# Gate and value products of a gated layer by Strassen's algorithm, with combined weights made early and streamed from DRAM

## The chip, the cores and the metric

The kernel runs on one core of one Trainium2 chip. The metric is the device time of one execution in microseconds (us). Every text below that speaks of an engine uses the profile's names: PE is TensorE (PEld its weight loads), DVE is VectorE, ACT is ScalarE, POOL is GpSimd, SP is SyncE, which here only issues DMAs.

## The reference: what is computed

Three stages, all in float32. Retention (linear attention with a decay) over q, k, v of 4 batches, 8 heads, 576 positions and head size 64 gives 2304 tokens of width 512. Two feed-forward layers follow:

```python
def _moe_ref(x, w_in, w_out):          # w_in 512 x 2048, w_out 2048 x 512
    h = x @ w_in
    sp = np.where(h > 20.0, h, np.log1p(np.exp(np.minimum(h, 20.0))))
    return (h * np.tanh(sp)) @ w_out
def _moe2_ref(x, w_gate, w_val, w_out):  # 512 x 1536, 512 x 1536, 1536 x 512
    g = x @ w_gate
    silu = g * (1.0 / (1.0 + np.exp(-g)))
    return (silu * (x @ w_val)) @ w_out
```

The weights arrive as 64-bit floats and are brought to 32 bits on the chip, two 32-bit words at a time.

## The kernel before

All the work of the two layers is cut into blocks of T = 384 tokens: 2304 tokens make NB = 6 blocks. Activations lie transposed, 128 features on the partitions and 384 tokens along the row. Every float32 operand of a matrix product is split into a rounded high part and a low remainder, each 32 bits wide, and a product is the sum of three: high by high, high by low, low by high. So `prod` (L424), which multiplies a 512 x 128 piece of weights with a block, issues 4 x 3 = 12 matmuls of 384 columns (L430).

**First layer.** `slot(s)` (L490) is one of 6 x 16 = 96 steps: `g1` makes 128 features of h for a block (12 matmuls), `mish` and `halves` (ACT activation, ACT cast, DVE subtraction) make and split the activation, and `g2` of four slots earlier (LAG = 4) adds its part to the block's result (12 matmuls, L464). The last slot of a block copies the result to `x2t[b]`.

**Second layer.** 6 x 12 = 72 steps (L565 on): `gv_prod` makes a gate and a value bank (24 matmuls), `silu` takes the activation on ACT (L537), multiplies on DVE (L540) and splits the product with `halves` (L486 on ACT, L487 on DVE), and `fin` of two steps earlier multiplies it with 128 rows of w_out, 9 matmuls of 512 columns (L551), into three banks that stand for a whole block. The last `g2` steps of the first layer stand between the first steps of the second. `split_x` splits the next block's activations at the end of each block.

**Weights.** `weights` (L132) takes one 512 KB raw piece through a chain: `fetch` (a DMA on SP's queue), `rebias` (ACT L102, DVE L103), `sign` (DVE L107), `join` (DVE L111), and `part` (ACT cast L125, POOL subtraction L126) into a resident tile. There are 32 pieces for the first layer, taken during retention and the first 17 slots, and 36 for the second, taken in the last two blocks of the first layer and the first eleven steps of the second, because a piece can only lie where one of the first layer has come free (pools `wa` with 19 and `wb` with 14 tiles of 4 KB a partition).

**Order.** The order on each engine is the order in the code (`manual_schedule`); each engine runs its own instructions in that order and waits on the others by semaphores. `pha` and `ph` are two banks each of PSUM, `acc` four; `bank` (L439) passes the four of `pha` and `ph` round.

Of the kernel before, what the change touches and what calls it, by code (L numbers as in the profile page):

```python
# [7 lines left out]
F32 = mybir.dt.float32  # L8
# [8 lines left out]
def retention_mish_swiglu(  # L17
# [35 lines left out]
    gp = ctx.enter_context(tc.tile_pool(name="gp", bufs=3))  # L53
    pha = ctx.enter_context(tc.tile_pool(name="pha", bufs=2, space=PSUM))


    def cols(w, i):
        return w.bitcast(U32)[:, i * 256:(i + 1) * 256].rearrange("(k p) f -> p k f", p=128)

    def rows(w, i):  # L60
        return w.bitcast(U32)[i * 128:(i + 1) * 128, :]
# [5 lines left out]
        if i >= OFF:  # L67
            todo.append(("out", i - OFF, rows(w1_out, i - OFF)))
    n1 = len(todo)
    for i in range(F2):  # L70
        todo.append(("gate", i, cols(w2_gate, i)))
        todo.append(("val", i, cols(w2_val, i)))
        todo.append(("fin", i, rows(w2_out, i)))

    NU = len(todo) - 3
    unit = {}
    pools = {"a": wa}
    raw = {}
# [2 lines left out]
    def words(j):  # L81
        w = raw[j].rearrange("p (n t) -> p n t", t=2)
        return w[:, :, 0], w[:, :, 1]
# [12 lines left out]
    def rebias():  # L96
        j = stage[1]
        if j >= stage[0]:
            return
        stage[1] += 1  # L100
        lo, hi = words(j)
        nc.scalar.activation(hi.bitcast(F32), hi.bitcast(F32), AF.Copy, scale=2.0 ** -112)  # L102
        nc.vector.tensor_scalar(lo, lo, 29, None, op0=ALU.logical_shift_right)  # L103
# [9 lines left out]
    def part(lim):  # L113
        j = stage[3]
        if j >= min(lim, stage[2]):
            return
        stage[3] += 1
        kind, i, _ = todo[j]
        where = "a" if j < NA else "b" if j < NA + NBU else "a" if j < 2 * NA + NBU else "b"
        if j < NU:  # L120
            u = pools[where].tile([128, 2, DM], F32R, tag="u", name=f"u{j}")
        else:
            u = xp.tile([128, 2, DM], F32R, tag="raw", name=f"u{j}", bufs=RAW)
# [8 lines left out]
    def weights(lim, late=False):  # L132
        j = stage[2]
        on = j < min(lim, stage[1])
        if on:
            sign(j)
        yield
        if late:
            part(lim)
        if stage[1] < seen[0]:  # L140
            rebias()
        seen[:] = seen[1], stage[0]
        yield
        if on:
            join(j)
            stage[2] += 1
        while not late and stage[3] < stage[2]:
            part(lim)
        fetch(lim + 3)
        seen[1] = stage[0]  # L150

    def run(step):
        for _ in step:
            pass

    xt = {}
    x2t = {}
    xs = {}
# [2 lines left out]
        d[j] = xp.tile([128, KT, T], F32, tag="x", name=f"{nm}{j}", bufs=5)  # L161

    def split_hi(d, nm, j, kk):
        s = xp.tile([128, 2, T], F32R, tag="xs", name=f"{nm}s{j}_{kk}", bufs=XS)
        nc.scalar.copy(out=s[:, 0, :], in_=d[j][:, kk, :])
        xs[nm, j, kk] = s

# [255 lines left out]
    with tc.manual_schedule():  # L423
        def prod(ps, u, nm, j):  # L424
            n = 3 * KT
            c = 0
            for kk in range(KT):
                s = xs[nm, j, kk]
                for a, e in ((0, 0), (0, 1), (1, 0)):
                    nc.tensor.matmul(  # L430
                        ps, lhsT=u[:, a, kk * 128:(kk + 1) * 128], rhs=s[:, e, :],
                        start=(c == 0), stop=(c == n - 1),
                    )
                    c += 1
# [55 lines left out]
        def slot(s):  # L490
            b, i = divmod(s, F1)
            if i == 0 and s:
                g2(s - LAG)
            g1(s)
            if s >= LAG and i:
                g2(s - LAG)
            d, nm, j = (xt, "x", b + 1) if b + 1 < NB else (x2t, "y", 0)
            parts = (i - F1 + 4,) if b and F1 - 4 <= i < F1 - 2 else range(2, KT) if i == F1 - 1 else ()
# [4 lines left out]
            lim = 0  # L503
            if s < F1 + OFF:
                lim = 0 if parts else n1
                while stage[3] < min(2 * s - OFF + 2 if s > OFF else s, n1):
                    run(weights(n1))
            elif b < NB - 1:
                lim = NA + NBU if i % 4 == 1 and b > 1 else 0
            elif i >= 2 and i % 6 != 5:  # L510
                lim = NA + NBU + 2 * i
# [4 lines left out]
            if lim:  # L516
                run(weights(lim, True))

        retention(slot)
        pools["b"] = ctx.enter_context(tc.tile_pool(name="wb", bufs=NBU, reuse_waits="tile"))  # L520
        pools["ph"] = ctx.enter_context(tc.tile_pool(name="ph", bufs=2, space=PSUM, reuse_waits="tile"))
        pools["acc"] = ctx.enter_context(tc.tile_pool(name="pacc", bufs=4, space=PSUM, reuse_waits="tile"))
        for s in range(2, NS):
            slot(s)


        def gv_prod(s):
            b, i = divmod(s, F2)
            ga, va = bank(f"ga{s}"), bank(f"va{s}")
            prod(ga, unit["gate", i], "y", b)  # L530
            prod(va, unit["val", i], "y", b)
            return ga, va

        def silu(s, ga, va):
            sg = gp.tile([128, T], F32, tag="w", name=f"sg{s}")
            more = stage[3] < len(todo)
            nc.scalar.activation(sg, ga, AF.Silu)  # L537
            if more:
                run(weights(len(todo)))
            nc.vector.tensor_tensor(out=sg, in0=sg, in1=va, op=ALU.mult)  # L540
            halves(sg, ("f", s))
            if more:
                run(weights(len(todo)))

        def fin(s):
            b, i = divmod(s, F2)
            if i == 0:
                accs["f", b] = [pools["acc"].tile([128, DM], F32, tag="acc", name=f"fa{b}_{d}") for d in range(TT)]
            u, g = unit["fin", i], gs.pop(("f", s))
            for m, a, e, c in order(TT, i == F2 - 1):  # L550
                nc.tensor.matmul(  # L551
                    accs["f", b][m], lhsT=g[:, e, m * 128:(m + 1) * 128], rhs=u[:, a, :],
                    start=(i == 0 and c == 0), stop=(i == F2 - 1 and c == 2),
                )
                if i == F2 - 1 and c == 2:
                    if m == 0:
                        ob = xp.tile([128, TT, DM], F32, tag="x", name=f"o{b}", bufs=5)
                    o = ob[:, m, :]
# [4 lines left out]
        NS2 = NB * F2  # L563
        nc.scalar.preload_act_table_set("silu_and_others")
        for s in range(NS2):  # L565
            b, i = divmod(s, F2)
            if s == 0:
                g2(NS - 4)
            pair = gv_prod(s)
            if s == 0:  # L570
                g2(NS - 3)
            elif s == 1:
                g2(NS - 2)
                g2(NS - 1)
                g2_out(NS - 1)
            silu(s, *pair)
            if s > 1:
                fin(s - 2)
            if b + 1 < NB and i >= F2 - 3:
                kk = i - (F2 - 3)  # L580
                if kk < 2:
                    split_x(x2t, "y", b + 1, kk, nc.vector)
                else:
                    split_x(x2t, "y", b + 1, 2, nc.vector)
                    split_x(x2t, "y", b + 1, 3, nc.vector)
        fin(NS2 - 2)
        fin(NS2 - 1)


# [56 lines left out]
```

## Time and profile before

| | us |
|---|---|
| median of three runs | 970.83 (970.68 to 971.12) |
| the profiled execution | 971.39 |
| its span in the trace | 969.6 |
| PE busy in the span | 949.1 (98%), 5900 matmuls |
| DVE busy | 366.6 (38%) |
| ACT busy | 320.5 (33%) |
| POOL busy | 139.9 (14%) |
| moved by DMA | 55.86 MB |

The page of the profile gives busy time by engine, the span in slices, the chain that ended last and the costliest groups of instructions. Matmuls overlap in the trace (one that is noted as 334 ns starts 173 ns behind the one before), so the pace of PE is read from the starts of successive groups in the timeline, not from the mean duration of one.

### The profile page before, as it was taken

How to read it: one execution, taken by the hardware profiler on the slowest of the kernel's cores; microseconds unless marked ns; L12 is line 12 of the kernel's file. 1: busy time of each engine (PE TensorE's matmuls, PEld its weight loads, DVE VectorE, ACT ScalarE, POOL GpSimd, SP SyncE). 2: the span in 40 equal slices, each digit the busy share in tenths (PEclk: the TensorE clock that was granted, in tenths of full speed). 3: DMA queues.
4: the chain of work that ended last, by engine and by line, in shares of the span. 5: the costliest groups of instructions: out<-in, count | busy, mean ns of one | idle time of the engine just before them, and what ended most of it. 6: DMA issues, size and time to landing. Idle time of an engine off the chain costs nothing.

```text
span 969.6 us, 14043 instructions
## 1 busy us (share of the span) xinstructions
PE 949.1 (98%) x5900; PEld 905.9 (93%) x5900; DVE 366.6 (38%) x575; ACT 320.5 (33%) x626; POOL 139.9 (14%) x102
## 2 busy tenths in 40 slices
PE   9898999999999999999999979999999999999998
PEld 8777899999999999999999969999999999999997
DVE  3997796212111112114686883122122122112211
ACT  4776564322322223224454542122112112112111
POOL 3765343000000000001333540000000000000000
PEclk9999999999999999999999999999999999999999
DMA  9999353000000000001334530000000000000000
GB/s 227 256 247 244 122 164 109 23 1 1 23 1 1 1 1 1 1 1 44 109 109 130 169 114 33 1 1 33 1 1 24 10 1 1 33 1 1 33 1 33
DMA packets 76848, 55.86 MB, mean 58 GB/s; under 512 B 41456, under 2 KB 70896, under 8 KB 76784
## 3 DMA queue, kind: packets, MB, share of 16 engines
q1 hardware_dynamic: 75680, 54.53, 20.5%
q8 instruction: 46, 0.75, 0.3%
q10 hardware_dynamic: 1104, 0.42, 0.2%
q14 instruction: 18, 0.15, 0.1%
HBM read 50.23 MB, written 4.72 MB: 57 GB/s over the span
## 4 chain that ended last, share of the span: by engine, by line
PE 86%; issue 3%; DVE 3%; DMA 3%; ACT 2%; POOL 2%; SPq 1%; POOLq 0%; DVEq 0%; ACTq 0%
PE h L430 21%; PE acc L464 21%; PE fa L551 14%; PE va L430 14%; PE ga L430 13%; DMA k<-in_k_dram 1%; POOL u L126 1%; PE o L356 1%; DVE raw L111 1%; DVE raw L107 1%; PE s L289 1%; PE idle L398 1%; DVE raw L103 1%; DMA raw<-in_moe_w_in_dram 1%; PE o L349 1%
## 5 line engine op out<-in xcount | busy, mean ns | idle before, releaser
L430 PE MATMUL h<-xs,u 128*128 128x384 f32 x1152 | 214.3, 334 | 0.0
L464 PE MATMUL acc<-g,u 128*128 128x384 f32 x1152 | 214.0, 334 | 0.0
L430 PEld LDWEIGHTS h<-xs,u 128*128 128x128 f32 x1152 | 200.8, 188 | 0.3 <-issue 0.2
L464 PEld LDWEIGHTS acc<-g,u 128*128 128x128 f32 x1152 | 201.0, 188 | 0.0
L430 PE MATMUL ga<-ys,u 128*128 128x384 f32 x864 | 165.2, 339 | 4.0 <-POOL u L126 2.2
L430 PEld LDWEIGHTS ga<-ys,u 128*128 128x128 f32 x864 | 154.6, 189 | 11.3 <-POOL u L126 2.8
L126 POOL TENSOR_TENSOR u<-raw,u 128x512 fp32r<-128x512 f32 x68 | 102.2, 1507 | 424.5 <-ACT u L125 397.7
L430 PE MATMUL va<-ys,u 128*128 128x384 f32 x864 | 161.9, 334 | 1.0 <-POOL u L126 1.0
L430 PEld LDWEIGHTS va<-ys,u 128*128 128x128 f32 x864 | 150.7, 188 | 1.6 <-POOL u L126 1.6
L487 DVE TENSOR_TENSOR g<-m,g 128x384 fp32r<-128x384 f32 x96 | 53.7, 559 | 255.8 <-ACT g L486 255.8
L540 DVE TENSOR_TENSOR sg<-sg,va 128x384 f32<-128x384 f32 x72 | 39.7, 552 | 260.8 <-PE va L430 260.8
L481 ACT ACTIVATE m<-h 128x384 f32<-128x384 f32 x96 | 47.3, 493 | 241.4 <-PE h L430 241.3
L537 ACT ACTIVATE sg<-ga 128x384 f32<-128x384 f32 x72 | 35.4, 492 | 174.9 <-PE ga L430 174.9
L125 ACT CAST u<-raw 128x512 fp32r<-128x512 f32 x68 | 44.9, 662 | 56.4 <-DVE raw L111 56.4
L103 DVE TENSOR_SCALAR raw<-raw 128x512 uint32<-128x512 uint32 x68 | 60.8, 895 | 1.6 <-DMA raw<-in_moe_w_out_dram 1.4
L107 DVE SCALAR_TENSOR_TENSOR raw<-raw 128x512 uint32<-128x512 uint32 x68 | 53.6, 788 | 0.0
L111 DVE SCALAR_TENSOR_TENSOR raw<-raw 128x512 uint32<-128x512 uint32 x68 | 51.0, 749 | 0.1
L486 ACT CAST g<-m 128x384 fp32r<-128x384 f32 x96 | 49.5, 515 | 2.5
L102 ACT ACTIVATE raw<-raw 128x512 f32<-128x512 f32 x68 | 46.8, 689 | 1.6 <-DMA raw<-in_moe_w_out_dram 0.9
L277 POOL TENSOR_TENSOR vs<-v,gv 128x512 f32<-128x512 f32 (+1 forms) x20 | 25.7, 1284 | 18.4 <-DMA v<-in_v_dram 14.1
L298 DVE TENSOR_TENSOR p<-s,mask 128x512 f32<-128x512 f32 (+1 forms) x40 | 23.5, 629 | 5.0 <-PE s L289 4.9
L356 PE MATMUL o<-p,vs 128*64 128x128 f32 (+1 forms) x320 | 21.3, 270 | 1.1 <-DVE p L298 1.0
(326 smaller groups left out, 682.8 us busy)
## 6 DMA issues: line engine op xcount, KB each, us to landing
raw<-in_moe_w_out_dram SPq DMA_DIRECT2D x28, 512.0 KB, 3.6
raw<-in_moe_w_in_dram SPq DMA_DIRECT2D x16, 512.0 KB, 5.2
raw<-in_moe_w_gate_dram SPq DMA_DIRECT2D x12, 512.0 KB, 3.6
raw<-in_moe_w_val_dram SPq DMA_DIRECT2D x12, 512.0 KB, 3.6
out_dram<-o SPq DMA_DIRECT2D x18, 256.0 KB, 2.3
q<-in_q_dram SPq DMA_DIRECT2D x8, 512.0 KB, 6.3
k<-in_k_dram SPq DMA_DIRECT2D x16, 256.0 KB, 5.8
v<-in_v_dram SPq DMA_DIRECT2D x16, 256.0 KB, 6.1
```

The source lines that it names most:

```text
L102: nc.scalar.activation(hi.bitcast(F32), hi.bitcast(F32), AF.Copy, scale=2.0 ** -112)
L103: nc.vector.tensor_scalar(lo, lo, 29, None, op0=ALU.logical_shift_right)
L107: nc.vector.scalar_tensor_tensor(lo, hi, 0x80000000, lo, op0=ALU.bitwise_and, op1=ALU.bitwise_or)
L111: nc.vector.scalar_tensor_tensor(lo, hi, 3, lo, op0=ALU.logical_shift_left, op1=ALU.bitwise_or)
L125: nc.scalar.copy(out=u[:, 0, :], in_=w)
L126: nc.gpsimd.tensor_tensor(out=u[:, 1, :], in0=w, in1=u[:, 0, :].bitcast(F32), op=ALU.subtract)
L430: nc.tensor.matmul(ps, lhsT=u[:, a, kk * 128:(kk + 1) * 128], rhs=s[:, e, :], start=(c == 0), stop=(c == n - 1),)
L464: nc.tensor.matmul(accs[b][d][:, :T], lhsT=u[:, a, d * 128:(d + 1) * 128], rhs=g[:, e, :], start=(i == 0 and c == 0), stop=(i == F1 - 1 an ...
L481: nc.scalar.activation(w, hs.pop(s), AF.Mish)
L486: nc.scalar.copy(out=g[:, 0, :], in_=x)
L487: nc.vector.tensor_tensor(out=g[:, 1, :], in0=x, in1=g[:, 0, :].bitcast(F32), op=ALU.subtract)
L551: nc.tensor.matmul(accs["f", b][m], lhsT=g[:, e, m * 128:(m + 1) * 128], rhs=u[:, a, :], start=(i == 0 and c == 0), stop=(i == F2 - 1 and ...
```

## The change

The gate and value products of two pieces of 128 features (e = 0, 1) and two blocks of tokens (h = 0, 1), each with the 512 rows of the sum cut into two halves of 256, are a 2 x 2 by 2 x 2 product of blocks. The changed kernel forms it with seven block products in place of eight (Winograd's form of Strassen's algorithm). A unit u of the second layer is such a pair of pieces for such a pair of blocks: 3 pairs of blocks x 6 pairs of pieces = 18 units, each with 7 products of 6 matmuls for the gate (z = 0) and 7 for the value (z = 1). Three banks t1, t2, t3 a half take turns in the two banks of `pha`; t1 and t2 and t3 are read by ACT or DVE in the middle of their accumulation, and p1, u and v are kept in SBUF.

The weights' side (a11, a12, a22 and four sums s1 to s4) is made in slots 20 to 82 of the first layer by `second`, in steps spread over five slots for each pair of pieces and side, split into high and low parts, written to DRAM and read back by `stream`, one 512 KB tile for two products, through nine buffers, anew for each pair of blocks. The activations' side (three parts as they are and four combinations) is made by `ysteps` on DVE and ACT: for the first pair of blocks in the last four slots of the first layer, for the others beside the last unit of the pair before. w_out's pieces go through DRAM too and are read once. The last four `g2` of the first layer run in a row. The matmuls of `fin` for unit u are handed out between the products of unit u + 1, two or three behind each product.

```diff
-    NA, NBU = 19, 14
+    NA, NBU = 19, 13
...
+    PREP = 20
...
-    wa = ctx.enter_context(tc.tile_pool(name="wa", bufs=NA))
+    cl, cr = ExitStack(), ExitStack()
+    wa = cr.enter_context(tc.tile_pool(name="wa", bufs=NA, side="right"))
...
+    def put(x, dst, nm, eng):
+        c = pools["c"].tile([128, 2, KH], F32R, tag="c", name=nm)
+        nc.scalar.copy(out=c[:, 0, :], in_=x)
+        eng.tensor_tensor(out=c[:, 1, :], in0=x, in1=c[:, 0, :].bitcast(F32), op=ALU.subtract)
+        nc.sync.dma_start(out=dst, in_=c.bitcast(F32))
...
+    def group(i, z, stg):
...
+        if stg == 3:
+            for out_, a, b, op in (
+                (s[1], v["a21"], v["a22"], ALU.add), (s[3], v["a11"], v["a21"], ALU.subtract),
+                (s[2], s[1], v["a11"], ALU.subtract), (s[4], v["a12"], s[2], ALU.subtract),
+            ):
+                nc.vector.tensor_tensor(out=out_, in0=a, in1=b, op=op)
+        for c, nm in enumerate(USES):
+            if (nm[0] == "a") == (stg == 3):
+                n = z * NG + c
+                put(v[nm] if nm[0] == "a" else s[int(nm[1])], comb[i][n // 2][:, n % 2], f"c{i}_{n}", nc.vector)
...
+    def second(s):
+        for n in range(2 * PAIRS):
+            t = s - PREP - 5 * n
+            if 0 <= t < 5:
+                group(n // 2, n % 2, t)
+            if 4 <= t < 8:
+                last(n, t - 4)
...
+        SA, SB = 4, 5
...
+        def stream(n):
...
+            su[n] = pools["sa" if n % (SA + SB) < SA else "sb"].tile([128, 2, 2, KH], F32R, tag="su", name=f"su{n}")
+            nc.sync.dma_start(out=su[n].bitcast(F32), in_=comb[n // NG % PAIRS][n % NG])
...
+        def ysplit(n, c, x):
+            y = pools["y"].tile([128, 2, KT // 2, T], F32R, tag="y", name=f"y{n}_{c}")
+            nc.scalar.copy(out=y[:, 0], in_=x)
+            nc.vector.tensor_tensor(out=y[:, 1], in0=x, in1=y[:, 0].bitcast(F32), op=ALU.subtract)
...
+        def ysteps(n):
...
+            ysplit(n, 0, b[1, 1])
+            minus(b[1, 1], b[1, 2], b[1, 1])
+            yield
...
+            minus(t2, b[2, 2], b[1, 1])
+            ysplit(n, 1, t2)
+            yield
+            ysplit(n, 2, b[2, 1])
+            minus(b[2, 1], b[2, 1], t2)
+            yield
+            minus(b[1, 2], b[2, 2], b[1, 2])
+            ysplit(n, 3, b[1, 2])
+            yield
+            ysplit(n, 4, b[1, 1])
+            yield
+            ysplit(n, 5, b[2, 1])
+            yield
+            ysplit(n, 6, b[2, 2])
+            yield
...
+            if s == NS - 5:
+                cr.close()
...
+                y0 = ysteps(0)
+            elif y0:
+                next(y0, None)
+                next(y0, None)
+        for s in range(NS - LAG, NS):
+            g2(s)
+            g2_out(s)
...
+        def strassen(u, z):
...
+            def result(e, h, bank_, part_):
+                if z == 0:
+                    x = pools["sg"].tile([128, T], F32, tag="sg", name=f"sg{u}_{e}{h}")
+                    if part_ is not None:
+                        add(x, bank_, part_)
+                    nc.scalar.activation(x, bank_ if part_ is None else x, AF.Silu)
+                    sg[u, e, h] = x
+                else:
+                    x = bank_
+                    if part_ is not None:
+                        x = pools["sg"].tile([128, T], F32, tag="cv", name=f"cv{u}_{e}{h}", bufs=2)
+                        add(x, bank_, part_)
+                    y = sg[u, e, h]
+                    nc.vector.tensor_tensor(out=y, in0=y, in1=x, op=ALU.mult)
+                    finish(u, e, h)
...
+            for c, (nm, tn, begin, end) in enumerate((
+                ("a11", 1, True, True), ("s2", 2, True, True), ("a12", 1, False, True), ("s3", 2, False, True),
+                ("s1", 3, True, True), ("a22", 2, False, True), ("s4", 3, False, True),
+            )):
+                if begin:
+                    t[tn] = pha.tile([128, T], F32, tag="h", name=f"t{u}_{z}_{tn}")
...
+                for kk in range(KT // 2):
+                    for a, x in ((0, 0), (0, 1), (1, 0)):
+                        nc.tensor.matmul(
+                            p, lhsT=w[:, n % 2, a, kk * 128:(kk + 1) * 128], rhs=y[:, x, kk, :],
...
+                if n % 2:
+                    stream(u * NG + n // 2 + SA + SB)
+                if c == 0:
...
+                    nc.scalar.copy(out=r["p1"], in_=p)
+                elif c == 1:
...
+                    add(r["u"], p, r["p1"])
+                elif c == 2:
+                    result(0, 0, p, None)
+                elif c == 3:
...
+                    add(r["v"], p, r["p1"])
+                elif c == 4:
+                    result(1, 1, p, r["v"])
+                elif c == 5:
+                    result(1, 0, p, r["p1"])
+                else:
+                    result(0, 1, p, r["u"])
+                fins(FINS[c])
+                if nexty and n >= 6:
+                    next(nexty[0], None)
...
+        FINS = (3, 2, 3, 2, 3, 2, 3)
```

`finish` calls `halves` on the product of silu and value and queues the nine `fin` matmuls of (e, h) for the next unit; `nexty` holds `ysteps` of the next pair of blocks in units 5 and 11.

## Rows read from the trace of the kernel before

**Rows 1.** The page: span; part 1, busy us, share, instructions.

```profile
span 969.6 us, 14043 instructions
PE 949.1 (98%) x5900; PEld 905.9 (93%) x5900; DVE 366.6 (38%) x575; ACT 320.5 (33%) x626; POOL 139.9 (14%) x102
```

**Rows 2.** Timeline of an undisturbed step of the second layer: start, us, engine, line, instructions.

```profile
704.74 2.27 PE L430 MATMUL ga<-ys,u 128*128 128x384 f32 x12
...
706.84 2.24 PE L430 MATMUL va<-ys,u 128*128 128x384 f32 x12
707.10 0.49 ACT L537 ACTIVATE sg<-ga 128x384 f32<-128x384 f32 x1 [3.07 <-PE ga L430]
...
708.92 2.24 PE L551 MATMUL fa<-u,g('f', 29)_6160 128*128 128x512 f32 x9
709.19 0.55 DVE L540 TENSOR_TENSOR sg<-sg,va 128x384 f32<-128x384 f32 x1 [4.57 <-PE va L430]
709.78 0.52 ACT L486 CAST g('f', 31)_6242<-sg 128x384 fp32r<-128x384 f32 x1 [2.19 <-DVE sg L540]
710.32 0.56 DVE L487 TENSOR_TENSOR g('f', 31)_6242<-sg,g('f', 31)_6242 128x384 fp32r<-128x384 f32 x1 [0.58 <-ACT g('f', 31)_6242 L486]
...
711.00 2.27 PE L430 MATMUL ga<-ys,u 128*128 128x384 f32 x12
```

**Rows 3.** Timeline of PE where the first layer ends and the second begins.

```profile
496.50 4.32 PE L464 MATMUL acc<-g,u 128*128 128x384 f32 x24
500.65 2.24 PE L430 MATMUL ga<-ys,u 128*128 128x384 f32 x12
...
559.05 2.27 PE L430 MATMUL ga<-ys,u 128*128 128x384 f32 x12
```

**Rows 4.** Timeline of PE where the second layer waits for its weights, and behind it.

```profile
568.22 2.01 PE L430 MATMUL ga<-ys,u 128*128 128x384 f32 x10 [1.39 <-POOL u L126]
...
576.28 0.62 PE L430 MATMUL ga<-ys,u 128*128 128x384 f32 x2 [1.89 <-ACT u L125]
...
577.67 3.38 PE L430 MATMUL ga<-ys,u 128*128 128x384 f32 x10 [0.77 <-POOL u L126]
...
585.67 2.27 PE L430 MATMUL ga<-ys,u 128*128 128x384 f32 x12
```

**Rows 5.** Stages: start:end, length, busy us (instructions) PE to POOL, granted clock, DMA share, GB/s.

```profile
200.00:300.00 100.00, 100.00 (x579) 100.00 (x578) 19.54 (x37) 28.82 (x60) 1.31 (x1) 1.00 0.02 6
...
564.00:568.00 4.00, 2.83 (x13) 1.94 (x11) 3.48 (x7) 2.49 (x5) 1.70 (x1) 1.00 0.69 243
...
576.00:578.00 2.00, 0.95 (x3) 0.63 (x4) 1.32 (x2) 1.21 (x3) 1.31 (x1) 0.82 0.00 0
578.00:580.00 2.00, 2.00 (x7) 2.00 (x7) 1.57 (x4) 0.34 (x1) 0.00 (x0) 0.50 0.00 0
580.00:582.00 2.00, 1.64 (x7) 1.33 (x7) 1.23 (x1) 1.23 (x3) 1.30 (x1) 0.83 0.00 0
```

**Rows 6.** DMA issues: KB each, median us from issue to landing.

```profile
raw<-in_moe_w_out_dram SPq DMA_DIRECT2D x28, 512.0 KB, 3.6
```

**Rows 7.** Groups by line and shape: busy us, mean ns of one, idle before.

```profile
L103 DVE TENSOR_SCALAR raw<-raw 128x512 uint32<-128x512 uint32 x68 | 60.8, 895 | 1.6 <-DMA raw<-in_moe_w_out_dram 1.4 <-DMA raw<-in_moe_w_val_dram 0.2
...
L125 ACT CAST u<-raw 128x512 fp32r<-128x512 f32 x68 | 44.9, 662 | 56.4 <-DVE raw L111 56.4
...
L165 ACT CAST ys<-y 128x384 fp32r<-128x384 f32 x24 | 11.7, 511 | 0.0
...
L369 DVE TENSOR_TENSOR x<-o,gout 128x512 f32<-128x512 f32 x14 | 9.6, 688 | 12.8 <-PE o L356 12.7
...
L369 DVE TENSOR_TENSOR x<-o,gout 128x256 f32<-128x256 f32 x8 | 3.2, 417 | 1.8 <-POOL gout L307 0.9 <-PE o L356 0.8
```

**Rows 8.** Timeline: the end of the kernel.

```profile
963.71 2.20 PE L551 MATMUL fa<-u,g('f', 71)_7948 128*128 128x512 f32 x9
```

**Rows 9.** Timeline: a DVE subtraction while POOL is at work (POOL 531.37, 1.32 us).

```profile
531.68 1.42 DVE L487 TENSOR_TENSOR g('f', 3)_4914<-sg,g('f', 3)_4914 128x384 fp32r<-128x384 f32 x1 [0.68 <-ACT g('f', 3)_4914 L486]
```

More of the change, by code (lines that the diff above doesn't have):

```diff
@@ L118, in part @@
         kind, i, _ = todo[j]
[L119 to L123, printed above, removed]
+        u = pools["a" if j < NA else "b"].tile([128, 2, DM], F32R, tag="u", name=f"u{j}")
         w = words(j)[0].bitcast(F32)
@@ L154, in run, with raw_load @@
             pass
+    NG = 7
+    PAIRS = F2 // 2
+    USES = ("a11", "s2", "a12", "s3", "s1", "a22", "s4")
+    KH = KT // 2 * 128
+    comb = [[dp.tile([128, 2, 2, KH], F32, tag=f"c{i}_{n}", name=f"comb{i}_{n}") for n in range(NG)] for i in range(PAIRS)]
+    find = [dp.tile([128, 2, DM], F32, tag=f"f{i}", name=f"find{i}") for i in range(F2)]
+    def raw_load(key, src, whole):
+        raw[key] = xp.tile([128, 2 * DM], U32, tag="raw", name=f"raw{key}", bufs=RAW)
+        nc.sync.dma_start(out=raw[key] if whole else raw[key].rearrange("p (k f) -> p k f", k=KT), in_=src)
@@ new lines, in last @@
+    def last(i, stg):
+        key = f"f{i}"
+        if stg == 0:
+            raw_load(key, rows(w2_out, i), True)
+        elif stg == 1:
+            rebias_raw(key)
+        elif stg == 2:
+            sign(key)
+            join(key)
+        else:
+            x = words(key)[0].bitcast(F32)
+            for h in range(DM // KH):
+                put(x[:, h * KH:(h + 1) * KH], find[i][:, :, h * KH:(h + 1) * KH], f"f{i}_{h}", nc.gpsimd)
+    def second(s):
[5 more added lines that the diff above has]
+                last(n, t - 4)
@@ L502, in slot @@
             halves(ws.pop(s), s)
-            lim = 0
             if s < F1 + OFF:
-                lim = 0 if parts else n1
-                while stage[3] < min(2 * s - OFF + 2 if s > OFF else s, n1):
+                while not parts and stage[3] < min(2 * s - OFF + 2 if s > OFF else s, n1):
                     run(weights(n1))
[L508 to L511, printed above, removed]
             for kk in parts:
@@ L515, in slot @@
                 g2_out(s - LAG)
-            if lim:
-                run(weights(lim, True))
+            if s < F1 + OFF and not parts:
+                run(weights(n1, True))
+            second(s)
         retention(slot)
-        pools["b"] = ctx.enter_context(tc.tile_pool(name="wb", bufs=NBU, reuse_waits="tile"))
+        pools["b"] = cl.enter_context(tc.tile_pool(name="wb", bufs=NBU, reuse_waits="tile"))
+        pools["c"] = cr.enter_context(tc.tile_pool(name="pc", bufs=4, side="right"))
@@ L523, in retention_mish_swiglu @@
+        y0 = None
         for s in range(2, NS):
             slot(s)
[L527 to L550, printed above, removed]
+            if s == NS - 5:
+                cr.close()
+                pools["y"] = ctx.enter_context(tc.tile_pool(name="yp", bufs=9, side="right", reuse_waits="tile"))
+                pools["sg"] = ctx.enter_context(tc.tile_pool(name="sg", bufs=5, side="right", reuse_waits="tile"))
+                pools["sa"] = ctx.enter_context(tc.tile_pool(name="sa", bufs=SA, side="right", reuse_waits="tile"))
+                for n in range(SA):
+                    stream(n)
+                y0 = ysteps(0)
+            elif y0:
+                next(y0, None)
+                next(y0, None)
@@ new lines, in retention_mish_swiglu @@
+        for s in range(NS - LAG, NS):
+            g2(s)
+            g2_out(s)
+        cl.close()
+        pools["sb"] = ctx.enter_context(tc.tile_pool(name="sb", bufs=SB, reuse_waits="tile"))
+        pools["fin"] = ctx.enter_context(tc.tile_pool(name="fp", bufs=F2, reuse_waits="tile"))
+        for n in range(SA, SA + SB):
+            stream(n)
+        fin_load(0)
+        fin_load(1)
+        nc.scalar.preload_act_table_set("silu_and_others")
+        sg = {}
+        ready = []
+        finq = []
@@ L551, in fin, with fins @@
+        def fins(count):
+            while count and finq:
+                u, e, h, m, a, x, first, final = finq.pop(0)
+                b = 2 * (u // PAIRS) + h
+                if first and m == 0:
+                    accs["f", b] = [
+                        pools["acc" if 3 * h + d < 4 else "ph"].tile(
+                            [128, DM], F32, tag="acc" if 3 * h + d < 4 else "h", name=f"fa{b}_{d}"
+                        ) for d in range(TT)
+                    ]
                 nc.tensor.matmul(
-                    accs["f", b][m], lhsT=g[:, e, m * 128:(m + 1) * 128], rhs=u[:, a, :],
```

119 lines of the change are left out of this document (83 added, 36 removed).

## The prediction

> **What bounds the kernel now.** I read the page first: PE is busy for 949.1 of 969.6 us, DVE for 38%, ACT for 33% [rows 1]. So the time follows PE's list of matmuls plus the few microseconds in which it waits. Then the timeline of one step of the second layer, for PE's pace: gate 704.74 to 706.84 (2.10 us for 12 matmuls), value to 708.92 (2.08), `fin` to 711.00 (2.08 for 9) [rows 2]. A matmul of 384 columns thus takes 0.1733 us in a run, a group of them that comes behind `fin` 0.02 to 0.03 us more, one of 512 columns 0.232. The same rows give the turnaround: DVE begins 0.27 us behind the start of the group that follows the value products (708.92, 709.19), ACT 0.04 behind DVE's end, DVE 0.02 behind ACT's. Third the border of the layers: `g2` of slots 91 and 92 takes 496.50 to 500.65, then the first gate group [rows 3]. Fourth, the one place where the second layer waits: from the group at 559.05 [rows 3] to that at 585.67 [rows 4] lie three steps, 3 x 6.26 = 18.8 us [rows 2], and they take 26.6. The 7.8 us more are waits for POOL's and ACT's part of the weights [rows 4] and a stretch at half clock behind them [rows 5]. The first row of the stage table shows PE without a gap in the first layer [rows 5].
>
> **The change, part by part, on the profiled execution's own span.**
>
> *Products.* Before: 72 steps x (2.10 + 2.08) = 301.0 us. After: 18 units x 14 products x 6 matmuls. In 17 units each product follows some `fin` matmuls, as the gate group does, so it costs 6 x 0.1733 + 0.027 = 1.067 (the gate group's 2.10 less the value group's 2.08, 0.02 to 0.03 with the rounding of the rows); unit 0 has no `fin` beside it, 1.04. Sum 17 x 14 x 1.067 + 14 x 1.04 = 268.5, a gain of **32.5 us**. If the extra does not come in such short runs, 1512 x 0.1733 = 262.0 and the gain is 39. The 648 `fin` matmuls stay, 150 us.
>
> *The wait for weights* goes: **-7.8 us**. All weights of the second layer are in DRAM by slot 83, and the first four tiles are fetched from slot 91 on, four slots of 4.16 and 8.3 us of `g2` ahead of use against 3.6 us for 512 KB from issue to landing [rows 6].
>
> *Making the combinations (slots 20 to 82, 62 x 4.16 = 258 us).* DVE: 36 raw pieces x 3 operations of at most 0.895 = 97 us; 48 sums and 84 subtractions of 256 columns at 0.417 = 55; the slots' own 62 x 0.56 = 35 [rows 2, 7]. 187 of 258 us. The fullest slot (four sums, three subtractions, its own) has 3.5 us for DVE in 4.16. ACT has less. What waits is `halves`, and PE wants it three slots (12.5 us) later; that is the cover. **0 us**; if DVE fell behind by more, each slot would cost the overhang, so 0 to 5. A gain is excluded, as PE has no gap there. On SP's queue, stores wait for DVE with only other stores and raw loads behind them.
>
> *The four `g2` in a row* move 2 x 4.17 us of products behind them, nothing more: the split of slot 95 is done 2.5 us after its `g1`, and is wanted after 8.3. **0 us.**
>
> *Handing the banks over.* Each product's bank is wanted back two products later, and a read by DVE or ACT stands between. That is new; no row shows it, so I lay the value half (z = 1) of a unit in queue order. Products end at 1.07, 2.84, 4.37, 6.14, 7.67, 9.44, 10.97, the half at 11.67. From product 4: add to 8.49, multiply to 9.04, cast on ACT to 9.60, subtract to 10.18; product 5's add to 10.73, its bank being wanted at 11.67; multiply 11.28, cast 11.84, subtract 12.42; product 6's add to 12.97, wanted at 13.44; multiply 13.52, cast 14.08; then ACT's copy p1 of the next unit, which stands behind that cast, to 14.57, wanted at 14.97. So every bank is back in time, with **0.4 us to spare** in a unit of 23.3, and the gate half has five DVE operations against thirteen, so nothing adds up. **0 us**, with 0 to 10 for the range: durations longer by 0.1 us would take up the spare. Unit 0 has no `fin` between its products: DVE's value half is 13 x 0.55 and four waits for the cast of 0.58, 9.5 us against 7.3. Laid out to the end of its effect it costs **+1.4 us** (0 to 3).
>
> *The activations' combinations in units 5 and 11.* From the gate half's last product on, 11 DVE operations of 768 columns join the queue and 7 casts on ACT. A DVE operation takes 0.417 us at 256 columns and 0.688 at 512 make 0.96 at 768; the cast, 0.511 at 384 and 0.662 at 512, makes 0.96 [rows 7]. DVE then has 13 x 0.55 + 11 x 0.96 = 17.7 us where PE has 11.67. Busy time alone puts PE 17.7 - 11.7 - 0.4 = 5.6 us back; with the four waits for casts (2.3) and half a microsecond for each of the seven new casts (3.5), 11.4. Laid out in queue order PE waits for 1.7, 0.8, 2.7, 1.5 and 1.7 us: 8.4, between the two, and I take it. Two such places (the first pair of blocks is done in the first layer): **+17 us**, 11 to 23. What is late there is always DVE's read of a bank.
>
> *The stream.* 126 tiles of 0.524 MB = 66 MB in some 437 us, 151 GB/s; a stretch of the kernel before moved 243 GB/s of such pieces at a DMA share of 0.69 [rows 5]. Nine buffers are 18 products, 30 us, ahead. **0 us.** Stores of results in units 6 and 12 add six copies to DVE and ACT: +0.2.
>
> *The end.* 36 `fin` matmuls (8.3 us) stand last in place of 18 [rows 8], and the first 27 cover the last product's add, multiply, cast and subtraction (2.5). 0 us.
>
> Sum: 969.6 - 32.5 - 7.8 + 1.4 + 17.0 + 0.2 = 947.9 us of span. The profiled execution took 971.39, 1.8 more than its span, and stands 0.56 above the median: 947.9 + 1.8 - 0.6 = **949 us**.
>
> **Rivals.**
>
> *A, as summed:* 943 to 957.
>
> *B, the combinations are cheaper:* lower ends of both unknown terms, 39 for the products and 11 for units 5 and 11: 936. For it: ACT's casts may run ahead of DVE. Against it: the alternation with the value half's own casts.
>
> *C, the spare 0.4 us is not there:* one DVE operation longer by 0.1 us moves product 6's add by 0.7. Laid out with 0.65 us for each, the layer costs 5 us more, with 0.75 16 more: 954 to 966. For it: a DVE subtraction beside POOL took 1.42 us in place of 0.56 [rows 9]. Against it: POOL has nothing to do in the second layer.
>
> *D, slower: the short waits bring PE's clock down.* Behind a wait of 1.89 us, 0.62 us of work and one of 0.77 [rows 4], the granted clock stood at 0.82, 0.50 and 0.83 in three stretches of 2 us [rows 5], that is 2.4 GHz and 1.2 GHz in turn, and (0.18 + 0.50 + 0.17) x 2 = 1.7 us were lost. The waits in units 5, 6, 11 and 12 are of that size; one such stretch in each is 7 us, and the forecast holds. It ends slower from 13 stretches on (22 / 1.7), so only if waits come in most units: two in each of 17 make 58 us, 1007. Against it: behind the wait of 1.39 us at 568 the clock stayed at full [rows 4]. The Trainium skill (TensorE: Matmul & The Clock Gate, A second HAM failure mode: psum-queue depth-cycling) says that a kernel whose PE idles briefly and often while it passes PSUM banks round has its clock swing between the two levels; by that rule D would be likely wherever C is true. One wait in the trace speaks for the rule, one against.
>
> *E, tiles of the stream come one at a time:* 126 x 3.6 = 454 us for the layer [rows 6] in place of 437: 966. Against it: 243 GB/s is more than the 146 of one 512 KB transfer in 3.6 us.
>
> That the seven products do not replace eight is excluded: they stand in the code.
>
> **How the numbers follow.** A 0.50, B 0.14, C 0.16, E 0.06, D 0.10, about as before for reasons not seen 0.04. The range reaches to B's 936 and to C's and E's 966. A measurement of this kernel can tell about 0.2% (2 us) from no change. Faster: A, B, C and E nearly whole, 0.85; same 0.05; slower 0.10.
>
> **What the profile after would show.** 1512 matmuls of products, in groups of six from start to start in 1.04 (extra absent) or 1.07 us. No wait of PE in units 2 to 4, 8 to 10 and 14 to 17: units of 23.3 us; any there is C. In units 5 and 11 five waits of 0.8 to 2.7 us, released by DVE's adds; none would be B. The granted clock at 1.00 apart from there. PE never waiting for a stream tile; if it does, E. The first layer without gaps. The prediction is wrong if PE waits in every unit, or if DVE's operations on PSUM take longer beside this traffic than in [rows 2].

## The result, and the profile after

The changed kernel takes 957.49 us (median of 957.2 to 960.54) against 970.84 for the kernel before on the same chip: a ratio of 0.9869, 95% interval 0.9849 to 0.989. It is faster by 13.3 us where 22 were forecast, so the time lies inside the range (936 to 966) and 8.5 us above its likeliest value.

The page of the changed kernel first: its span, its busy times and the DMA issue of the stream (KB each, median us from issue to landing); they answer [rows 1] and [rows 6].

```profile
span 955.4 us, 14669 instructions
...
PE 918.8 (96%) x5684; PEld 869.6 (91%) x5684; DVE 518.9 (54%) x896; ACT 360.8 (38%) x731; POOL 109.3 (11%) x90
...
su<-comb SPq DMA_DIRECT2D x126, 512.0 KB, 3.3
```

PE lost 216 matmuls (5900 to 5684) and 30.3 us of busy time, but the span fell by 14.2 only: PE now waits more. The stage table of the changed kernel tells where. Its two stages are the first layer from slot 20 on and the second layer (start:end, length, busy us of PE, PEld, DVE, ACT, POOL, granted clock, DMA share, GB/s).

```profile
181.20:515.52 334.32, 328.16 (x1874) 326.14 (x1873) 182.71 (x354) 150.19 (x330) 23.02 (x24) 0.99 0.46 153
515.52:951.40 435.88, 422.51 (x2161) 388.08 (x2160) 204.37 (x358) 104.57 (x202) 0.00 (x0) 1.00 0.49 165
```

The second layer takes 435.9 us; the prediction's working gave 437. In the first layer PE is idle for 6.2 us and part of the time at half clock, where the kernel before had no gap at all, as its own stage from slot 20 to the end of the first layer shows:

```profile
181.00:500.60 319.60, 319.60 (x1846) 319.60 (x1845) 87.22 (x141) 102.26 (x208) 19.88 (x12) 1.00 0.06 19
```

The timeline of PE at the border of the layers shows how late the second one starts:

```profile
505.11 10.56 PE L544 MATMUL acc<-g,u 128*128 128x384 f32 x60
515.52 15.28 PE L749 MATMUL t<-y,su 128*128 128x384 f32 x84
531.27 1.32 PE L749 MATMUL t<-y,su 128*128 128x384 f32 x6 [0.48 <-DVE cv L719]
```

In the kernel before three `g2` still stood behind the first gate product, so by [rows 3] the same point of the work was reached there at 500.65 + 3 x 2.08 = 506.9; here it is reached at 515.5. From the first product of slot 2 on (111.58 us before, 110.18 after) this piece takes 395.3 us before and 405.3 after: **10.0 us are lost in the first layer**, in which not a matmul was changed. It is no accident of one execution: e3 to e7 below leave that code as it is up to the layer's last slots, and the same piece takes 404.4 to 405.7 us in their traces.

The starts of PE's groups, slot by slot, against those of the kernel before put the loss in four places: 1.3 us at slot 32, 4.7 at slots 48 to 53, 0.1 at slot 68 and 3.2 at slot 80; 0.6 more comes in steps of 0.03. Slots 32, 48, 64 and 80 begin the blocks of tokens, and in slots 52 and 68 the first `g2` of a new block stands. Two timelines of the changed kernel show what happens there. The first has the work of slots 49 to 51 in the queues of DVE, SP and ACT, and PE in slot 52:

```profile
311.62 0.82 DVE L177 TENSOR_TENSOR c<-rawv,c 128x256 fp32r<-128x256 f32 x2 [0.50 <-ACT c L176]
...
312.07 0.80 SPq L178 DMA_DIRECT2D comb<-c  x2
...
312.92 0.44 SPq L171 DMA_DIRECT2D rawf<-in_moe_w_out_dram  x1
...
313.42 1.28 SPq L171 DMA_DIRECT2D rawg<-in_moe_w_gate_dram  x2
...
318.76 0.69 ACT L103 ACTIVATE rawf<-rawf 128x512 f32<-128x512 f32 x1 [5.84 <-DMA rawf<-in_moe_w_out_dram]
319.36 0.48 ACT L561 ACTIVATE m<-h 128x384 f32<-128x384 f32 x1
319.87 0.51 ACT L566 CAST g<-m 128x384 fp32r<-128x384 f32 x1
320.29 0.85 ACT L554 COPY y<-acc 128x384 f32<-128x384 f32 x2
...
320.81 3.07 PE L544 MATMUL acc<-g,u 128*128 128x384 f32 x12 [2.37 <-ACT y L554]
```

ACT stands for 5.8 us at `rebias` of a w_out piece (L103). The load of that piece is issued at 312.92, just when ACT has come to it: on SP's queue it stands behind the stores of the combinations of the same step, and the last of these goes out when DVE's subtraction ends (311.62 + 0.82). So it is for all twelve w_out pieces: the load is issued 0.4 us behind the last store of the step, and it lands 3.7 to 6.0 us later, 4.8 at the median by the DMA table:

```profile
rawf<-in_moe_w_out_dram SPq DMA_DIRECT2D x12, 512.0 KB, 4.8
```

Behind the `rebias` in ACT's queue wait the next slot's activation and the copy of the finished block out of its banks (L554), and PE cannot start the next block's `g2` until those banks are free. Behind the wait the stage table gives a granted clock (a share of full speed) of 0.57, that is 2.4 GHz and 1.2 GHz in turn:

```profile
316.00:322.00 6.00, 3.63 (x22) 3.10 (x20) 2.02 (x5) 3.20 (x7) 0.00 (x0) 1.00 0.57 198
322.00:326.00 4.00, 4.00 (x15) 4.00 (x15) 3.93 (x7) 1.93 (x5) 2.16 (x2) 0.57 0.00 0
```

The second timeline is slot 80, where the next block's activations are wanted:

```profile
441.60 1.09 DVE L177 TENSOR_TENSOR c<-rawv,c 128x256 fp32r<-128x256 f32 x3
...
442.60 0.55 DVE L567 TENSOR_TENSOR g<-m,g 128x384 fp32r<-128x384 f32 x1
443.07 1.02 DVE L250 TENSOR_TENSOR xs<-x,xs 128x384 fp32r<-128x384 f32 x2
443.68 3.23 PE L510 MATMUL h<-xs,u 128*128 128x384 f32 x17 [2.14 <-DVE xs L250]
```

Here DVE was in the middle of sums and subtractions for the combinations (four operations before 441.60, three more here), and the split of the next block (L250) stood behind them. The wait behind slot 32 is of the first kind: ACT stood for a load until 232.20, and the splits behind it were late.

In the second layer the units take 23.2 us, apart from units 0 and 1 and 5, 6, 11 and 12 (and 23.4 in units 7 and 13). The timeline of unit 5's value half, where PE waits longest:

```profile
648.24 0.96 DVE L619 TENSOR_TENSOR y<-y,y 128x768 fp32r<-128x768 f32 x1 [0.95 <-ACT y L618]
649.11 0.55 DVE L719 TENSOR_TENSOR v<-t,p 128x384 f32<-128x384 f32 x1
...
649.72 1.99 PE L749 MATMUL t<-y,su 128*128 128x384 f32 x6 [2.37 <-DVE v L719]
```

The add that frees the bank (v) stands behind a subtraction of 768 columns which itself waited for ACT's cast: what the prediction laid out.

### The profile page after: what moved, and what is told of

Read it like the earlier page. It is cut to its first block, busy times and chain, and to the rows that moved or that the text cites. A ratio compares the mean times of both kernels' runs of the same rounds, so it can differ in the third digit from the quotient of the medians.

```text
span 955.4 us, 14669 instructions
## 1 busy us (share of the span) xinstructions
PE 918.8 (96%) x5684; PEld 869.6 (91%) x5684; DVE 518.9 (54%) x896; ACT 360.8 (38%) x731; POOL 109.3 (11%) x90
## 4 chain that ended last, share of the span: by engine, by line
PE 72%; DMA 9%; DVE 9%; ACT 4%; SPq 2%; issue 2%; POOL 1%; DVEq 0%; ACTq 0%
PE t L749 26%; PE h L510 15%; PE fa L689 15%; PE acc L544 15%; DMA k<-in_k_dram 3%; DMA rawf<-in_moe_w_out_dram 2%; DMA comb<-c 2%; DMA rawv<-in_moe_w_val_dram 1%; DVE y L619 1%; SPq L300 1%; DVE g L567 1%; ACT y L618 1%; DMA rawg<-in_moe_w_gate_dram 1%; DVE c L177 1%; DVE rawv L108 1%
## 5 line engine op out<-in xcount | busy, mean ns | idle before, releaser
L749 PE MATMUL t<-y,su 128*128 128x384 f32 x1512 | 308.5, 340 | 13.4 <-DVE v L719 4.7
L749 PEld LDWEIGHTS t<-y,su 128*128 128x128 f32 x1512 | 271.7, 188 | 40.1 <-DVE cv L719 7.1
L567 DVE TENSOR_TENSOR g<-m,g 128x384 fp32r<-128x384 f32 x96 | 53.7, 559 | 100.1 <-ACT g L566 98.6
L726 ACT ACTIVATE sg<-sg 128x384 f32<-128x384 f32 x54 | 28.4, 525 | 98.8 <-DVE sg L719 98.8
L123 POOL TENSOR_TENSOR u<-raw,u 128x512 fp32r<-128x512 f32 x32 | 47.1, 1473 | 62.1 <-ACT u L122 60.3
L177 POOL TENSOR_TENSOR f<-rawf,f 128x256 fp32r<-128x256 f32 x24 | 23.0, 979 | 262.5 <-ACT f L176 262.5
L719 DVE TENSOR_TENSOR v<-t,p 128x384 f32<-128x384 f32 x36 | 20.0, 557 | 45.5 <-PE t L749 44.6
L104 DVE TENSOR_SCALAR raw<-raw 128x512 uint32<-128x512 uint32 x32 | 37.7, 1178 | 0.0
L734 DVE TENSOR_TENSOR sg<-sg,cv 128x384 f32<-128x384 f32 x54 | 30.2, 558 | 1.9
L122 ACT CAST u<-raw 128x512 fp32r<-128x512 f32 x32 | 21.2, 662 | 22.3 <-DVE raw L112 22.2
L103 ACT ACTIVATE rawf<-rawf 128x512 f32<-128x512 f32 x12 | 8.3, 689 | 56.5 <-DMA rawf<-in_moe_w_out_dram 56.5
L108 DVE SCALAR_TENSOR_TENSOR raw<-raw 128x512 uint32<-128x512 uint32 x32 | 26.2, 818 | 0.0
L112 DVE SCALAR_TENSOR_TENSOR raw<-raw 128x512 uint32<-128x512 uint32 x32 | 26.1, 816 | 0.0
```

Source lines behind the costliest of these rows:

```text
L108: nc.vector.scalar_tensor_tensor(lo, hi, 0x80000000, lo, op0=ALU.bitwise_and, op1=ALU.bitwise_or)
L177: eng.tensor_tensor(out=c[:, 1, :], in0=x, in1=c[:, 0, :].bitcast(F32), op=ALU.subtract)
L567: nc.vector.tensor_tensor(out=g[:, 1, :], in0=x, in1=g[:, 0, :].bitcast(F32), op=ALU.subtract)
L719: nc.vector.tensor_tensor(out=out_, in0=a, in1=b_, op=ALU.add)
L749: nc.tensor.matmul(p, lhsT=w[:, n % 2, a, kk * 128:(kk + 1) * 128], rhs=y[:, x, kk, :], start=begin and kk == 0 and (a, x) == (0, 0), stop ...
```

## The experiments

All start from the changed kernel and are compared with it (957.5) and with the kernel before on the same chip. The kernel before took 971.48 us beside e1 to e4 and 971.03 beside e5 to e8, against 970.84 beside the changed kernel, so I take a difference from 957.5 to be good to about 1 us (an estimate); lengths of stretches are from the traces.

**e1, the block borders kept clear.**

```diff
+    SKIP = (2, 14)
+    done = [0]
...
-            second(s)
+            if i not in SKIP:
+                if s >= PREP:
+                    second(PREP + done[0])
+                    done[0] += 1
```

> One edit: the making of the combinations skips the slots i = 2 and i = 14 of every block, so that nothing of it stands in the queues of ACT and DVE ahead of the splits of the next block's activations (slot 15) and of the copies of the block's result (slot 3). Theory 'border': the first layer lost some 9.9 us in four places, all at block borders, because ACT waited there for a raw load or DVE was in the middle of the combinations; with the slots clear nearly all of it returns, 948 to 950 us, and PE has no gap above 0.3 us between slots 20 and 91. Rival 'load': the loss comes from the sheer traffic and the busy share of DVE and ACT, which stays the same; then 956 to 958.

Measured: 949.15 us (947.97 to 949.63), 8.3 less. The stage table of this kernel from slot 20 to the end of the first layer's usual order has PE busy throughout, with DVE and ACT busy as long as in the changed kernel (183 and 150 us) and the traffic unchanged:

```profile
181.00:505.80 324.80, 324.80 (x1872) 324.80 (x1872) 183.35 (x354) 150.28 (x329) 22.95 (x24) 1.00 0.48 158
```

From slot 2 to the second layer it takes 396.0 us, 9.3 less than the changed kernel and 0.7 more than the kernel before. The amount of work and traffic is the same, and a slot that has a step of `second` has one as before; the 63 steps end in slot 90 in place of 82. ACT still waits 46.3 us for w_out's loads (56.5 in the changed kernel, see e2), and PE waits for nothing:

```profile
ACT rawf L103 <- DMA rawf<-in_moe_w_out_dram: 46.3, 12, 5.8
```

So the rival "load" falls, the border is shown.

**e2, w_out's pieces loaded one slot earlier.**

```diff
-            if 4 <= t < 8:
+            if t == 3:
+                last(n, 0)
+            if 5 <= t < 8:
                 last(n, t - 4)
```

> One edit: w_out's raw piece is fetched one slot earlier than it is now, so two slots ahead of its use on ACT in place of one; all other work stands where it was. Theory 'border by a late load': ACT, which waited 56 us in all for these 12 loads, no longer does; the losses at slots 32/33 (1.4 us) and 48 to 54 (5.0 with the stretch at half clock) go, the one at slot 80/81 (3.2 us), where DVE stands in the middle of sums and subtractions, stays: 950 to 953 us. Rival 'DVE's work ahead of the border': the loads were not what was late, 956 to 958.

Measured: 953.29 us (951.88 to 954.46), at the upper edge of what was expected. The table of waits of ACT in the first layer (engine, line and what it waited for: us in all, times, longest), first of the changed kernel,

```profile
ACT rawf L103 <- DMA rawf<-in_moe_w_out_dram: 56.5, 12, 6.0
...
ACT rawv L103 <- DMA rawv<-in_moe_w_val_dram: 2.6, 4, 0.8
...
ACT rawg L103 <- DMA rawg<-in_moe_w_gate_dram: 1.2, 2, 0.7
```

then of e2:

```profile
ACT rawv L103 <- DMA rawv<-in_moe_w_val_dram: 22.3, 12, 3.6
ACT rawg L103 <- DMA rawg<-in_moe_w_gate_dram: 18.5, 10, 5.5
ACT rawf L103 <- DMA rawf<-in_moe_w_out_dram: 8.2, 9, 1.8
```

and PE's waits in e2:

```profile
PE h L512 <- DVE xs L252: 2.6, 3, 2.1
PE acc L546 <- ACT y L556: 0.7, 1, 0.7
```

ACT hardly stands for w_out's pieces any more, but it now stands for those of gate and value: 49.0 us in all against 60.3. What moved is the place of the wait. From slot 2 to the second layer the kernel takes 400.9 us, so 4.5 us of the 9.3 come back. The loss at slot 32 and the wait of 2.4 us for the copy in slot 52 are gone, with no half clock; the wait of 0.7 for the copy is a new one, at 386.85 in slot 68, behind the load of a value piece. The wait of 2.1 for DVE's split at slot 80 stays, and at slot 48 0.6 us more are lost to the split.

By place, then, a late load cost 5.7 of the 9.3 us in the changed kernel (slots 32, 52 and 53, the half clock with it) and DVE's work ahead of the split 3.5 (slots 80 and 48). The first share is shown by e2; for the second no experiment took DVE's work away by itself, it rests on the timeline of slot 80, on e1 and on what e2 leaves.

**e3, the activations' combinations handed out singly.** The order of the operations becomes split 0, b11, t2, split 1, b12, split 2, split 3, b21, splits 4 to 6, each with a `yield` of its own, and t2 lies in a buffer of the raw pieces, which is free in the second layer. The first pair of blocks, in the first layer, takes three a slot in place of two steps.

```diff
-                if nexty and n >= 6:
+                if nexty and n in YAT[u % PAIRS]:
                     next(nexty[0], None)
...
+        YAT = {PAIRS - 1: (0, 1, 2, 3, 4, 7, 8), 0: (0, 1, 2, 3)}
```

> One edit: the combinations and splits of the activations for the second and third pair of blocks are handed out singly, five operations in the gate half of unit 5 (11), two in its value half, four in the gate half of unit 6 (12), in place of all beside unit 5's value half; the number of operations is the same. Theory 'late DVE in units 5 and 11': the 17 us that PE waits there (and one stretch at half clock, 1.6) go nearly wholly: by the same laying out in queue order the layer falls by 16.8, so 939 to 942 us. Rival 'the work itself': DVE's 21 us of extra work must be paid somewhere in units 5, 6, 11 and 12, since the spare time in a unit is 0.4 us: then half or less returns, 949 or more.

Measured: 941.78 us (940.03 to 942.47), 15.7 less. Units 5, 6, 11 and 12 take 23.27, 23.20, 23.30 and 23.19 us; in the changed kernel they took 29.99, 24.73, 29.74 and 24.98. The stage table of this kernel over the stretch in which unit 5 gives way to unit 6, and again for 11 and 12:

```profile
639.00:663.00 24.00, 24.00 (x126) 22.38 (x125) 15.35 (x25) 8.73 (x15) 0.00 (x0) 1.00 0.48 157
786.00:810.00 24.00, 24.00 (x126) 22.29 (x125) 14.95 (x26) 7.90 (x15) 0.00 (x0) 1.00 0.58 193
```

So placed, nine of the eleven steps in gate halves and two at the start of a value half, the same operations cost nothing. DVE's five operations of a gate half take 2.8 of its 11.6 us; the 0.4 us to spare is a matter of the value half's later products alone.

**e4, the combinations left out in units 5 and 11** (all pairs of blocks use the first pair's activations).

```diff
-            if u % PAIRS == PAIRS - 1 and u + 1 < NS2:
-                nexty.append(ysteps(u // PAIRS + 1))
...
-                y = ys[n0, c]
+                y = ys[0, c]
```

> Leaves out part of the computation: the combinations of the activations are made for the first pair of blocks alone, and all three pairs are multiplied with those. It prices that work in units 5 and 11 by itself. Theory: 17 us of waits and 1.6 us of half clock go, 938 to 941 us; units 5 and 6 take 23.2 us like the others. Rival, if the waits there had another cause (stores of results, the stream): they stay, 952 or more.

Measured: 942.16 us (939.02 to 944.4), a little above what was expected, but from the first product of unit 0 to the last matmul 419.05 us in the trace, against 435.66 in the changed kernel and 419.19 in e3. So that work costs 16.6 us where it stands and 0.1 where e3 puts it.

**e5 and e6, one and two DVE operations more in the chain.**

```diff
+            if (e, h) in AGAIN:
+                g = gs[u, e, h]
+                nc.vector.tensor_tensor(out=g[:, 1, :], in0=x, in1=g[:, 0, :].bitcast(F32), op=ALU.subtract)
...
+        AGAIN = ((1, 1),)
```

In e6 `AGAIN` is ((1, 1), (1, 0)).

> One DVE subtraction of the value half (that of the result (1,1), behind product 4) is done twice, 0.5 us more in the chain that hands the banks on; the output is the same. Theory 'spare 0.4 us': the chain laid out in the prediction has 0.4 us to spare, so a steady unit goes from 23.2 to 23.2 or 23.3 us, and with units 0, 1, 6, 7, 12 and 13, which have no spare, the kernel gains 2 to 4 us: 959 to 962. Rival 'slack is wide' (DVE has 13 us free in a unit of 23): no change at all, also with two. Rival 'no slack': 0.5 us in each of 17 units, 966.

> Two DVE subtractions of the value half (those of the results (1,1) and (1,0)) are done twice, 1.0 us more in the chain. Theory 'spare 0.4 us': the second half microsecond cannot be hidden; a steady unit goes from 23.2 to 23.8 us with PE waiting for the add behind product 6, and the kernel to 967 to 971 us, though DVE stays busy for little over half of the layer. Rival 'slack is wide': 957 to 959.

Measured: 964.0 us (962.41 to 964.86) and 973.47 (972.06 to 975.07), both above what was expected; steady units take 23.42 and 24.01 us. If each operation more lengthens the chain by d and x is to spare, d - x = 0.22 and 2d - x = 0.81, so d = 0.59 and x = 0.37. The spare is as laid out (0.4); the operation was priced too low, at 0.5. The timeline of e5 has it: the repeated subtraction (L709) starts 0.60 behind the first (L567).

```profile
577.11 0.56 DVE L567 TENSOR_TENSOR g(2, 1, 1)_5904<-sg,g(2, 1, 1)_5904 128x384 fp32r<-128x384 f32 x1 [0.58 <-ACT g(2, 1, 1)_5904 L566]
...
577.71 0.56 DVE L709 TENSOR_TENSOR g(2, 1, 1)_5904<-sg,g(2, 1, 1)_5904 128x384 fp32r<-128x384 f32 x1
```

In e6 PE waits in every unit for the add behind product 6, as the timeline shows, and the granted clock of four units with such waits stays at 1.00:

```profile
582.35 0.55 DVE L723 TENSOR_TENSOR cv<-t,u 128x384 f32<-128x384 f32 x1
...
582.96 1.32 PE L753 MATMUL t<-y,su 128*128 128x384 f32 x6 [0.49 <-DVE cv L723]
```

```profile
535.00:640.00 105.00, 103.01 (x527) 94.01 (x528) 46.75 (x86) 22.23 (x45) 0.00 (x0) 1.00 0.55 187
```

With DVE busy for 46.75 of 105 us, two operations of 0.56 us a unit cost 14.6 us of the layer and the whole gain: e6 is no faster than the kernel before (ratio 1.002, 1.0005 to 1.0034).

**e7, half as much again read by the stream.**

```diff
             nc.sync.dma_start(out=su[n].bitcast(F32), in_=comb[n // NG % PAIRS][n % NG])
+            if n % 2 and n > SA + SB:
+                more = xp.tile([128, 2 * DM], U32, tag="raw", name=f"more{n}", bufs=RAW)
+                nc.sync.dma_start(out=more.bitcast(F32), in_=comb[n // NG % PAIRS][n % NG].rearrange("p a b c -> p (a b c)"))
```

> Every second tile of the stream is read from DRAM a second time, into a buffer that nobody reads: some 33 MB more in the second layer, 227 GB/s in place of 151. Theory 'the stream is hidden': no change, 956 to 959 us, units 23.2 us. Rival 'the stream presses' (on PE's pace, on DVE's operations or on the arrival of the tiles): units longer than 23.3 us or PE waiting for tiles, 962 or more.

Measured: 956.93 us (956.77 to 959.57); the units take what they took. The stage table of a stretch, of e7 and then of the changed kernel:

```profile
560.00:640.00 80.00, 80.00 (x416) 74.46 (x415) 34.23 (x61) 17.60 (x35) 0.00 (x0) 1.00 0.76 268
```

```profile
560.00:640.00 80.00, 80.00 (x415) 74.41 (x415) 34.07 (x61) 17.72 (x36) 0.00 (x0) 1.00 0.54 189
```

The stream is hidden, with room for 79 GB/s more; the number of matmuls in the stretch and DVE's busy time don't move.

**e8, the edits of e1, e2 and e3 together.**

> The edits of e1, e2 and e3 together. They act in different layers, so by the theory their gains add: 957.5 less 8.3 to 9.3 for the clear borders, less 15.7 to 17 for the spread combinations: 931 to 933.5 us, no gap of PE above 0.3 us between slot 20 and the end except the three of units 0 and 1 (0.5 to 0.8 us each). Rival, if one cure only moved a wait: 937 or more.

Measured: **931.82 us** (931.35 to 933.74), a ratio of 0.9589 to the kernel before (0.9564 to 0.9613). The gains add: 957.5 - 931.8 = 25.7, against 8.3 + 15.7 = 24.0 one by one. Two stages of it, the first layer and the steady part of the second:

```profile
180.00:505.00 325.00, 325.00 (x1873) 325.00 (x1872) 184.28 (x354) 152.29 (x331) 22.44 (x24) 1.00 0.48 157
...
530.00:925.00 395.00, 395.00 (x2036) 365.75 (x2035) 190.87 (x337) 96.94 (x187) 0.00 (x0) 1.00 0.48 162
```

PE is without a gap in both; what is left are the three short waits of units 0 and 1, which no experiment tried to remove.

## Why the prediction was right, and where it was not

**The sum, term by term.**

| term | laid out | measured |
|---|---|---|
| a steady unit (84 product, 36 `fin` matmuls) | 23.3 us | 23.20 |
| wait for weights in the second layer | gone, -7.8 | PE waits for no tile of the stream |
| units 0 and 1, no `fin` between the products | +1.4 | +1.3: gaps of 0.47, 0.82 and 0.57 us between starts, less 0.17 each |
| units 5, 6, 11, 12 | +17.0 | +16.6 |
| second layer in all | 437 | 435.9 |
| making the combinations in the first layer | 0 (0 to 5) | +10.0 |
| work ahead of slot 2, not touched | 0 | -1.4 |

So the second layer, where nearly all of the reasoning went, came out to 0.3%, and the miss is the first layer's: of the 8.5 us, 7.5 are span (955.4 against 947.9), the 10.0 less what came out shorter. The -1.4 is chance: the kernel before had a stretch at half clock at 86 us and the changed kernel none there, and in the runs from e1 to e8 slot 2 begins anywhere from 110.1 to 111.9 us. It hid a part of the miss.

**The step that failed** is the term for the making of the combinations, with the cover that was named for it: "What waits is `halves`, and PE wants it three slots (12.5 us) later; that is the cover." That holds for `halves`, but two other pieces of work stand in the same queues and have less time: the split of the next block's last two parts, made in slot 15 and wanted by the next slot's products, and the copy of the finished block, whose banks the next block's first `g2` wants. Both stand in `slot`, beside the `halves` that the step reasons about. The step asked how busy DVE was in the fullest slot and not which instruction behind it is wanted first, and its count of that slot has no split in it (1.02 us for two in the timeline of slot 80). It priced ACT by its busy time ("ACT has less"), and on SP's queue it saw "only other stores and raw loads" behind the stores that wait for DVE, and priced the raw loads at nothing; ACT stood 56.5 us for them. Most of that cost nothing, as e1 shows, but at the borders it cost more than half of the loss (5.7 us, the half clock with it). The upper bound of 5 us, drawn from busy time, was therefore too low for a cost of 10.0. e1 shows the place and e2 the late loads; what DVE's work costs by itself is read from the timeline. That the time lies in the range all the same is owed to the room left for C and E, which did not come.

**Handing the banks over** was laid out with 0.4 us to spare; e5 and e6 give 0.37. Rival C was thus false for this kernel, but by little: one operation of 0.56 us more in the value half costs 5.1 us of the layer (e5).

**Units 5 and 11** went as laid out in queue order: 1.7, 0.8, 2.7, 1.5 and 1.7 us were expected, and the gaps from start to start between PE's matmuls in units 11 and 12, less the 0.17 to 0.23 of an ordinary one, are 1.75, 0.75, 2.55, 1.3 and 1.5. Rival B was the wrong reading of the same queue. That the work could be had for nothing was not seen in the prediction: it counted DVE's free time in the value half (0.4 us) and not in the gate half.

**The clock (rival D)** fell where the waits were long. In unit 5 the stage table shows one stretch at half clock behind the wait of 2.4 us, and none in unit 11 with the same waits:

```profile
640.00:650.00 10.00, 5.55 (x26) 4.15 (x25) 7.53 (x11) 3.64 (x5) 0.00 (x0) 1.00 0.33 111
650.00:653.50 3.50, 3.50 (x12) 3.31 (x12) 2.71 (x5) 1.25 (x2) 0.00 (x0) 0.51 0.00 0
...
788.00:800.00 12.00, 7.57 (x37) 6.07 (x36) 8.92 (x14) 4.32 (x7) 0.00 (x0) 1.00 0.26 88
```

It cost nothing there: units 5 and 6 together are as long as units 11 and 12 (54.72 us both), because PE had to wait for DVE anyway, and one of its waits went. In e7 the stretch stood in unit 11 and none in unit 5, and the pairs take 54.72 and 54.71 us. In the first layer the stretch behind the wait of 2.4 us (slots 52 and 53) was paid in full. In e6, where that code is the same, the same wait stood without it; PE's timeline, first of the changed kernel,

```profile
320.81 3.07 PE L544 MATMUL acc<-g,u 128*128 128x384 f32 x12 [2.37 <-ACT y L554]
323.68 3.25 PE L510 MATMUL h<-xs,u 128*128 128x384 f32 x12
326.76 2.24 PE L544 MATMUL acc<-g,u 128*128 128x384 f32 x12
```

then of e6:

```profile
320.66 2.47 PE L544 MATMUL acc<-g,u 128*128 128x384 f32 x12 [2.41 <-ACT y L554]
322.97 2.28 PE L510 MATMUL h<-xs,u 128*128 128x384 f32 x12
325.09 2.28 PE L544 MATMUL acc<-g,u 128*128 128x384 f32 x12
```

From the one `g2` to the next it is 5.95 us against 4.43, so the stretch cost 1.5 us of the 10.0. From slot 2 to the last matmul no kernel of this case has a stretch at half clock but behind waits of 1.9 to 2.4 us, and not behind all of these. One short wait a unit left the clock at 1.00 in the four units of e6 shown above. The rule of the Trainium skill (TensorE: Matmul & The Clock Gate, A second HAM failure mode: psum-queue depth-cycling) is of a kernel whose PE idles briefly and frequently between groups of matmuls and whose clock swings by it. Here one wait in 24 us (e6) shows no swing, and four or five waits within 15 us (units 5 and 11) show one stretch at most; no run waits more often than that, so this case neither bears the rule out nor refutes it.

**The stream (rival E)** is refuted: 165 GB/s over the layer in the changed kernel, 268 in a stretch of e7.

## What to carry to other kernels

Work that is added to an engine with time to spare is free only if no instruction behind it in the same queue is wanted soon: go through the queue and write down, for each instruction, when its result is wanted, and look above all at the borders of blocks, where short deadlines meet. The queue that issues DMAs belongs to this: a load that stands behind a store is issued no sooner than the work that the store waits for is done. An engine's busy share says little of this, on either side: ACT was busy for less than half of the first layer and held PE up by waiting for a load, and DVE was busy for less than half of the second and two operations more undid the whole gain. When the queue is laid out in order, with durations from neighbouring rows, the waits come out to a tenth of a microsecond or two, and the same layout tells where the work would cost nothing.

## What the runs showed of the hardware that was not expected

Loads of 512 KB from issue to landing take 3.6 us at the median in [rows 6], but 4.8 at the median and up to 6.0 us for the w_out pieces of the changed kernel's first layer, all but the last of them the first of three loads in a row, right behind stores of 256 KB each; why they take longer no run shows. A stretch at half clock cost nothing in units 5 and 6, where PE was not the one that was late, and 1.5 us in the first layer. The tiles of the stream, 4 KB to a partition, arrive 3.3 us behind their issue while DVE's operations keep their durations (0.55 to 0.56 us at 384 columns, 0.96 at 768) with 165 to 268 GB/s moving into the same memory.
